# Splitting and reordering the opening of a fused Linformer attention and quick-GELU feed-forward kernel, and moving one later projection

## Chip, cores, metric

One core of a Trainium2 chip. The metric is the device time of one execution in microseconds (us), median of several runs. The span of a profile (first to last instruction) is some 1.8 us shorter than the time of the same run. All runs used here are of the fast state, but for run 5, a single run whose state is unknown; each also lists the mean clock that the matrix engine (PE) was granted.

## The reference

Eight batches, eight heads, 1024 tokens, head size 64; k and v are projected along the sequence to 64 rows.

```python
k_proj = einsum('ks,bhsd->bhkd', E, k)
v_proj = einsum('ks,bhsd->bhkd', F, v)
attn   = softmax(q @ k_proj.T / sqrt(64))
x      = (attn @ v_proj)            # heads side by side: 8192 x 512
h      = x @ w_in                   # 512 -> 2048
out    = (h * sigmoid(1.702 * h)) @ w_out
```

## The kernel before

The output is made in 16 blocks of 512 tokens. For each block, `ffn1` runs 16 chunks (`fc`) of the first matrix, `ffn2` four row groups of the second. The attention of later blocks is filled in between, by a table of slots: `at(j, slot, f)` runs `f` after chunk `slot` of block `j`; `O` = 16 is the first slot of the `ffn2` part. Two places matter: the opening, ahead of the first `ffn1`, and the projections of batch 3 in block 3.

```python
nc.sync.dma_start(out=ef_f[:KP], in_=E)
nc.scalar.dma_start(out=ef_f[KP:], in_=F)
load_kv(k, kt, 0, "k_sb", H // 2)              # GpSimd queue, fp32 -> bf16
...
load_kv(q, qt, 0, "q0_sb", H, 0, 2)
load_kv(v, vt, 0, "v_sb", ((0, 4), (4, 2), (6, 2)))
load_kv(q, qt, 0, "q0_sb", H, 2, 2)
for i in range(6):
    load_w_in(i)
...
def proj(b):                                   # reads k_sb and v_sb of batch b
    ...
def kv_out(b):
    def go():
        ...
        nc.vector.tensor_copy(k_b, ps[LO])
        if b > 1:
            nc.sync.dma_start_transpose(out=kts[b % 2], in_=k_b...)   # k' for the scores
        v_out(b, ps, 0, HP)
...
def warm(n):                                   # matmuls on zeros: keep PE's clock up
    w_ps = f_tile([P, TB])
    for _ in range(n):
        nc.tensor.matmul(w_ps, zeros[:, :P], zeros, start=True, stop=True)
...
at(2, O + 5, sums(4))                          # reciprocals, out to DRAM, broadcast back
at(3, 6, proj(3), kv_out(3), values(4, 0))
...
for j in range(3, NBLK - 1):
    for u in range(2):
        if j + 3 < NBLK:
            at(j, O + 6 * u, scores(j + 3, u)) # block 3: first use of k' of batch 3
...
for j in range(NBLK):
    if j % NB2 == 0 and j // NB2 + 2 < B:
        load(j // NB2 + 2)                     # k, q, v of a later batch into single buffers
```

The buffers of the loaded k, q and v are single. So the loads of a later batch wait for the reads of the one before.

The softmax here doesn't subtract the row's maximum and nothing guards it: scores larger than these inputs give would overflow.

Of the kernel before, what the change touches and what calls it, by code (L numbers as in the profile page):

```python
# [10 lines left out]
BF16 = mybir.dt.bfloat16  # L11
AF = mybir.ActivationFunctionType
# [5 lines left out]
def kernel(ctx, tc, q, k, v, E, F,  # L18
# [5 lines left out]
    P = 128  # L24
# [55 lines left out]

    nc.sync.dma_start(out=ef_f[:KP], in_=E)
    nc.scalar.dma_start(out=ef_f[KP:], in_=F)
    load_kv(k, kt, 0, "k_sb", H // 2)
    ident = consts.tile([P, P], BF16)
    make_identity(nc, ident)
    load_kv(q, qt, 0, "q0_sb", H, 0, 2)
    load_kv(v, vt, 0, "v_sb", ((0, 4), (4, 2), (6, 2)))
    load_kv(q, qt, 0, "q0_sb", H, 2, 2)
    for i in range(6):
        load_w_in(i)  # L90
    load_kv(q, qt, 0, "q0_sb", H, JB, JB)
    for i in range(6, 8):
# [14 lines left out]
    ones = consts.tile([P, D], BF16)  # L107
    nc.vector.memset(ones, 1.0)

    vxs = []  # L110
    for i in range(2):
        vx = consts.tile([P, H, D + 1], BF16, name=f"vx{i}")
        nc.vector.memset(vx, 0.0)
        for r, xs_ in ((LO, X_LO), (HI, X_HI)):
            nc.vector.memset(vx[r].rearrange("k (u x) d -> k u x d", x=4)[:, :, xs_, D:], 1.0)
        vxs.append(vx)

    def f_tile(shape, dt=F32):
        return ps_f.tile(shape, dt, name="f_ps")

    def warm(n):
# [3 lines that stand above are left out]
# [1 line left out]
    warm(12)  # L126
    nc.vector.tensor_copy(ef_sb[:, :S // 2], ef_f[:, :S // 2])
    nc.scalar.copy(ef_sb[:, S // 2:], ef_f[:, S // 2:])
    eft = consts.tile([P, J, 2 * KP], BF16, name="eft")
    efv = ef_sb.rearrange("k (p j) -> k j p", j=J)  # L130
    t_ps = f_tile([P, J, 2 * KP], BF16)
    for j in range(J):
        nc.tensor.transpose(t_ps[:, j, :], efv[:, j, :], ident)
    nc.vector.tensor_copy(eft, t_ps)
    warm(4)


    kvps, kbs, qT, expT, xT, rbc = {}, {}, {}, {}, {}, {}
# [1 line left out]
    def proj(b):  # L140
        def go():
            kvps[b] = f_tile([P, H, D])
            for j in range(J):
                for e, r in enumerate((LO, HI)):
                    nc.tensor.matmul(kvps[b][r], eft[:, j, e * KP:(e + 1) * KP],  # L145
                                     (kt, vt)[e][b][:, :, j, :],
                                     start=(j == 0), stop=(j == J - 1))
        return go

    def proj0(e, h0, n):  # L150
        ps = f_tile([P, n, D])
        for j in range(J):
            nc.tensor.matmul(ps, eft[:, j, :], (kt, vt)[e][0][:, h0:h0 + n, j, :],  # L153
                             start=(j == 0), stop=(j == J - 1))
        return ps

    def k_half(k_ps, g):
        k_b = att.tile([KP, H // 2, D], BF16, name="k0_b")
        nc.vector.tensor_copy(k_b, k_ps[LO])
        k_tr(0, k_b, 2 * g)  # L160

    def k_tr(b, k_b, p0):
        n = k_b.shape[1] // 2
# [3 lines left out]
                                ident[:KP, :KP])  # L167
        nc.vector.tensor_copy(kts[b % 2][:, p0:p0 + n, :], t_ps)

    def v_out(b, v_ps, p0, n, cp=nc.vector.tensor_copy):  # L170
        if b < 2:
            if n == 1:
                for r, t in ((LO, p0 % 2), (HI, 1 - p0 % 2)):
                    cp(vxs[b][r, 2 * p0 + t, :D], v_ps[HI, t, :])
            else:
                vv = v_ps[HI].rearrange("k (u x) d -> k u x d", x=4)
                vx = vxs[b][:, 2 * p0:2 * (p0 + n), :D].rearrange("k (u x) d -> k u x d", x=4)
                for r, xs_ in ((LO, X_LO), (HI, X_HI)):
                    cp(vx[r, :, xs_], vv[:, :, xs_])
        if b > 0:  # L180
            vv = v_ps[HI].rearrange("k (u x) d -> k u x d", x=4)
            for r, xs_ in ((LO, X_LO), (HI, X_HI)):
                nc.vector.tensor_copy(vqs[b % 2][r].rearrange("k (u e) d -> k u e d", e=2), vv[:, :, xs_, :])

    def kv_out(b):
        def go():
            ps = kvps.pop(b)
            k_b = att.tile([KP, H, D], BF16, name="k_b")
            nc.vector.tensor_copy(k_b, ps[LO])  # L189
            if b > 1:  # L190
                nc.sync.dma_start_transpose(out=kts[b % 2], in_=k_b.rearrange("k h d -> k (h d)"))
            v_out(b, ps, 0, HP)
            kbs[b] = k_b
        return go

    def q_tr(b, g):
        def go():
            if g == 0:
                qT[b] = att.tile([P, J, HP, P], BF16, name="qT")
            t_ps = f_tile([P, 2, HP, P], BF16)  # L200
            for jj in range(2):
                for h in range(H):
                    r = h % 2 * D
                    nc.tensor.transpose(t_ps[r:r + D, jj, h // 2, :], qt[0][:, h, 2 * g + jj, :], ident)  # L204
            nc.vector.tensor_copy(qT[b][:, 2 * g:2 * g + 2], t_ps)
        return go

    def q_dma(b, j0=0, n=J):
# [16 lines left out]
    def scores(h, u, half=None):  # L225
        b, c = divmod(h, NB2)
        j0, n = (c * JB, JB) if half is None else (c * JB + half * JB // 2, JB // 2)
        ts = slice(j0 * P - c * TB, (j0 + n) * P - c * TB)

        def go():  # L230
            if h not in expT:
                expT[h] = att.tile([P, HP, TB], BF16, name="expT", bufs=3)
            s_ps = [f_tile([P, n * P]) for _ in range(2)]
            eight(s_ps, [kts[b % 2][:, 2 * u + i, :] for i in range(2)],
                 [qT[b][:, j0:j0 + n, 2 * u + i, :] for i in range(2)])
            for i in range(2):
                nc.scalar.activation(expT[h][:, 2 * u + i, ts], s_ps[i], AF.Exp, scale=scale)  # L237
        return go
# [54 lines left out]
    def tok(h, p, half):  # L293
        def go():
            d_ps = f_tile([P, 4, D + 1]) if (h, half) == (0, 0) and p > 1 else                 ps_d.tile([P, 4, D + 1], F32, name="d_ps")
            for i in range(2):
                t = 2 * half + i
                nc.tensor.matmul(d_ps[:, 2 * i:2 * i + 2, :].rearrange("s t d -> s (t d)"),  # L298
                                 expT[h][:, p, t * P:(t + 1) * P],
                                 vxs[h // NB2][:, 2 * p:2 * p + 2].rearrange("r t d -> r (t d)"),  # L300
                                 start=True, stop=True)
            rd = work.tile([P, 4, 1], F32, name="rd")
            nc.vector.reciprocal(rd, d_ps[:, :, D:])
            xs[h, p, half] = work.tile([P, 4, D], BF16, name="x_sb", bufs=4)
            nc.vector.tensor_tensor(xs[h, p, half], d_ps[:, :, :D], rd.to_broadcast([P, 4, D]), op=ALU.mult)  # L305
        return go
# [14 lines left out]
    def ffn1(j, fc, ts=slice(0, TB)):  # L321
        if j not in gts:
            gts[j] = work.tile([P, FC, TB], BF16, name="gT")
        n = ts.stop - ts.start
        h_ps = f_tile([P, n])
        for kc in range(KC):
            nc.tensor.matmul(h_ps, w_in_sb[:, kc, fc * P:(fc + 1) * P], xT[j][:, kc, ts],  # L327
                             start=(kc == 0), stop=(kc == KC - 1))
        if j > 0 or ts.start > 0 or fc > 3:
            nc.scalar.activation(gts[j][:, fc, ts], h_ps, AF.Gelu_apprx_sigmoid)  # L330
        else:

            t_sb = work.tile([P, n], F32, name="t_sb", bufs=3)
            nc.scalar.activation(t_sb, h_ps, AF.Tanh, scale=0.851)
            g = gts[j][:, fc, ts]
            nc.vector.scalar_tensor_tensor(g, t_sb, 1.0, h_ps, op0=ALU.add, op1=ALU.mult)
            nc.vector.tensor_scalar_mul(g, g, 0.5)
# [32 lines left out]
    def at(j, slot, *fs):  # L370
        fill.setdefault((j, slot), []).extend(fs)

    O = FC
    Q = 2 * FC
    for g in range(2):
        k_half(proj0(0, 4 * g, 4), g)
        warm(3)
    q_tr(0, 0)()
    warm(2)
    v_out(0, proj0(1, 0, 4), 0, 2)  # L380
    for u in range(2):
        scores(0, u, 0)()
    for p in range(2):
        tok(0, p, 0)()
    v_out(0, proj0(1, 4, 2), 2, 1)
    x_tr(0, 0, 0)()
    v_out(0, proj0(1, 6, 2), 3, 1, nc.scalar.copy)
    tok(0, 2, 0)()
    x_tr(0, 1, 0)()
    tok(0, 3, 0)()  # L390
    x_tr(0, 2, 0)()
    q_tr(0, 1)()
    x_tr(0, 3, 0)()

    order = [(half, fc) for fcs in (range(12), range(12, FC)) for half in range(2) for fc in fcs]
    at(0, 0, scores(0, 0, 1))
    at(0, 1, scores(0, 1, 1))
    for p in range(HP):
        at(0, 5 + p, tok(0, p, 1))
        at(0, 8 + p, x_tr(0, p, 1))  # L400
    at(0, 20, q_tr(0, 2))
    at(0, 23, q_tr(0, 3))
    at(0, 3, gelu_table)
    for u in range(2):
        at(0, Q + u, scores(1, u))
    at(0, Q + 1, gelu_table)
# [20 lines left out]
    at(2, 11, norm(3, 1))  # L427
    at(2, O + 5, sums(4))
    at(2, O, q_dma(3))
    at(3, 6, proj(3), kv_out(3), values(4, 0))  # L430
    for b in range(4, B):
        j = NB2 * b - 4
        at(j, O + 6, proj(b), kv_out(b))
# [59 lines left out]
```

## Time and profile before

| | before |
|---|---|
| median time, us | 513.48 (512.97 to 514.33, 4 runs) |
| span of the profile | 513.4 |
| PE busy | 497.8 us, 97% |
| PE idle | 6.2 us in the first 30 us; 9.4 us after, of which 3.2 at the very end and 1.1 in the wait below |
| PE at half clock | from 7.3 us to past 10.4 us |

A row of the stage view gives the stretch, its length, busy us (and instructions) of PE, weight loads, VectorE (DVE), ScalarE (ACT) and GpSimd (POOL), then the granted clock, the DMA share and GB/s. In a timeline row the brackets at the end say how long the engine had been idle and what ended that.

### The profile page before, as it was taken

What the parts mean: (1) busy time and instruction counts of PE and PEld (TensorE: products, weight loads), DVE (VectorE), ACT (ScalarE), POOL (GpSimd) and SP (SyncE); (2) the same over time, 40 slices, a digit from 0 to 9 for tenths busy, and PEclk for the clock granted to TensorE, in tenths of its full rate; (3) what the DMA queues carried; (4) which work ended last, traced back from release to release, by engine and by line L of the source; (5) the groups of instructions that cost most, each with busy time, mean ns of one, the idle gap of its engine ahead of it and who ended that gap; (6) DMA issues with size and microseconds to landing.
All of it is one profiled execution on the core that took longest, in us unless ns stands there. A gap on an engine that the chain in (4) does not pass through costs nothing.

```text
span 513.4 us, 7127 instructions
## 1 busy us (share of the span) xinstructions
PE 497.8 (97%) x3022; PEld 231.1 (45%) x3072; DVE 165.0 (32%) x203; ACT 262.5 (51%) x439; POOL 77.3 (15%) x96
## 2 busy tenths in 40 slices
PE   6899999999999999999999999999999999999997
PEld 3585445434434444444444444444444444444444
DVE  2542224765261621416242241615214161511000
ACT  1476454555537456372655627375473737344351
POOL 6442051060510051000510023000000000000000
PEclk8999999999999999999999999999999999999999
DMA  9999989999899389670997339990602305050102
GB/s 168 197 202 207 212 121 165 191 150 161 195 179 245 44 148 211 135 172 15 224 170 184 73 78 215 126 235 12 170 1 63 103 1 165 1 165 1 82 0 83
DMA packets 124737, 67.64 MB, mean 132 GB/s; under 512 B 92273, under 2 KB 116081, under 8 KB 122785
## 3 DMA queue, kind: packets, MB, share of 16 engines
q0 software_dynamic: 84384, 29.37, 51.0%
q1 hardware_dynamic: 40240, 37.56, 29.7%
q8 instruction: 24, 0.39, 0.3%
q10 hardware_dynamic: 80, 0.26, 0.2%
q14 instruction: 9, 0.07, 0.0%
HBM read 71.83 MB, written 16.97 MB: 173 GB/s over the span
## 4 chain that ended last, share of the span: by engine, by line
PE 93%; DMA 3%; issue 1%; DVE 1%; ACT 1%; ACTq 0%
PE f_ps L359 42%; PE f_ps L327 42%; PE f_ps L145 3%; PE f_ps L222 2%; DMA kt<-k_b 2%; PE n_ps L222 1%; DMA ef_f<-in_E_dram 1%; PE f_ps L124 1%; PE n_ps L313 1%; PE f_ps L153 1%; PE d_ps L298 1%; PE d_ps L256 1%; PE f_ps L204 0%; PE f_ps L351 0%; DVE x_sb L305 0%
## 5 line engine op out<-in xcount | busy, mean ns | idle before, releaser
L327 PE MATMUL f_ps<-xT,w_in_sb 128*128 128x512 bf16 (+1 forms) x1071 | 225.8, 366 | 1.1
L359 PE MATMUL f_ps<-w_out_sb,gT 128*128 128x512 bf16 x976 | 221.0, 379 | 4.1 <-issue 3.6
L330 ACT ACTIVATE gT<-f_ps 128x512 bf16<-128x512 f32 (+1 forms) x268 | 151.2, 575 | 64.6 <-PE f_ps L327 63.6
L327 PEld LDWEIGHTS <-w_in_sb 128*128 128x128 bf16 x1088 | 105.3, 98 | 115.8 <-issue 2.1
L359 PEld LDWEIGHTS <-gT 128*128 128x128 bf16 x1008 | 95.7, 98 | 120.4 <-issue 11.3
L362 ACT COPY o_sb<-f_ps 128x512 f32<-128x512 f32 x63 | 36.9, 586 | 128.5 <-PE f_ps L359 117.9
L286 DVE TENSOR_TENSOR xT<-n_ps,rbc 128x512 bf16<-128x512 f32 x48 | 30.9, 686 | 211.3 <-PE n_ps L222 123.0
L259 DVE RECIPROCAL rden<-d_ps 128x512 f32<-128x512 f32 x24 | 78.7, 3322 | 7.8 <-PE d_ps L256 7.8
L64 POOL DMA_DIRECT2D q_sb<-in_q_dram x56 | 49.1, 904 | 59.1 <-DMA k_sb<-in_k_dram 39.0
L237 ACT ACTIVATE expT<-f_ps 128x512 bf16<-128x512 f32 (+1 forms) x68 | 35.2, 572 | 37.7 <-PE f_ps L222 37.7
L58 POOL DMA_DIRECT2D k_sb<-in_k_dram x9 | 7.8, 863 | 172.0 <-PE f_ps L145 151.7
L237 ACT ACT_TABLE_LOAD x13 | 16.7, 1283 | 5.9 <-PE f_ps L222 5.7
L241 ACT ACT_TABLE_LOAD x14 | 18.0, 1283 | 0.3
L189 DVE CAST k_b<-f_ps 64x512 bf16<-64x512 f32 x7 | 4.8, 681 | 36.7 <-PE f_ps L145 36.7
L222 PE MATMUL f_ps<-qT,kt 64*32 64x512 bf16 (+1 forms) x272 | 13.7, 374 | 1.5 <-DMA kt<-k_b 1.1
L276 DVE RECIPROCAL rdn<-d_ps 128x512 f32<-128x512 f32 x4 | 13.4, 3352 | 5.0 <-PE d_ps L222 5.0
L145 PE MATMUL f_ps<-k_sb,eft 128*64 128x512 bf16 x56 | 13.4, 382 | 0.0
L145 PE MATMUL f_ps<-v_sb,eft 128*64 128x512 bf16 x56 | 13.4, 382 | 0.0
L353 DVE COPY o_sb<-f_ps 128x256 f32<-128x256 f32 x1 | 0.4, 425 | 38.6 <-issue 38.6
L222 PEld LDWEIGHTS <-kt 64*32 64x32 bf16 x272 | 3.9, 88 | 15.5 <-issue 13.8
L222 PE MATMUL n_ps<-expT,vq 64*32 64x512 bf16 x208 | 10.4, 378 | 0.0
L305 DVE TENSOR_TENSOR x_sb<-d_ps,rd 128x256 bf16<-128x256 f32 x22 | 9.3, 425 | 0.8
(59 smaller groups left out, 123.3 us busy)
## 6 DMA issues: line engine op xcount, KB each, us to landing
out_dram<-o_sb SPq DMA_DIRECT2D x15, 1024.0 KB
rbc<-rdr SPq DMA_DIRECT2D x24, 512.0 KB
k_sb<-in_k_dram POOLq DMA_DIRECT2D x7, 1024.0 KB, 14.2
v_sb<-in_v_dram POOLq DMA_DIRECT2D x7, 1024.0 KB, 10.4
q_sb<-in_q_dram POOLq DMA_DIRECT2D x56, 128.0 KB, 14.4
w_in_sb<-in_moe_w_in_dram POOLq DMA_DIRECT2D x8, 256.0 KB, 12.5
w_out_sb<-in_moe_w_out_dram POOLq DMA_DIRECT2D x4, 512.0 KB, 14.7
k_sb<-in_k_dram POOLq DMA_DIRECT2D x2, 512.0 KB, 7.7
```

The costliest lines, as they stand in the source:

```text
L64: nc.gpsimd.dma_start(out=qt[b][:, j], in_=qv[:, j])
L145: nc.tensor.matmul(kvps[b][r], eft[:, j, e * KP:(e + 1) * KP], (kt, vt)[e][b][:, :, j, :], start=(j == 0), stop=(j == J - 1))
L222: nc.tensor.matmul(outs[i][r.start + c:r.start + c + 32], lhsTs[i][ri, c:c + 32], rhss[i][ri], start=True, stop=True)
L237: nc.scalar.activation(expT[h][:, 2 * u + i, ts], s_ps[i], AF.Exp, scale=scale)
L241: nc.scalar.preload_act_table(AF.Gelu_apprx_sigmoid)
L259: nc.vector.reciprocal(rden[:, e, :], d_ps[e])
L276: nc.vector.reciprocal(rd, d_ps[i])
L286: nc.vector.tensor_tensor(x_of(h)[:, 2 * u + i, :], n_ps[i], rbc[h][:, 2 * u + i, :], op=ALU.mult)
L327: nc.tensor.matmul(h_ps, w_in_sb[:, kc, fc * P:(fc + 1) * P], xT[j][:, kc, ts], start=(kc == 0), stop=(kc == KC - 1))
L330: nc.scalar.activation(gts[j][:, fc, ts], h_ps, AF.Gelu_apprx_sigmoid)
L359: nc.tensor.matmul(o_ps[n], gts[j][:, fc, n * P:(n + 1) * P], w_out_sb[:, fc, :], start=(fc == 0), stop=(fc == FC - 1))
L362: nc.scalar.copy(osb[j][:, n, :], o_ps.pop(n))
```

## The change

The intent is a shorter latency chain before the first `ffn1`. The core of the diff (the mask, the tiles for v' and the q units are cut):

```diff
 nc.scalar.dma_start(out=ef_f[KP:], in_=F)
-load_kv(k, kt, 0, "k_sb", H // 2)
+nc.scalar.preload_act_table(AF.Exp)
+load_kv(k, kt, 0, "k_sb", ((0, 4), (4, 2), (6, 2)))
 ...
 load_kv(v, vt, 0, "v_sb", ((0, 4), (4, 2), (6, 2)))
+load_w_in(0)
 load_kv(q, qt, 0, "q0_sb", H, 2, 2)
-for i in range(6):
+for i in range(1, 6):
     load_w_in(i)
 ...
+def v_piece(h0, n):
+    v_ps = proj0(1, h0, n)
+    vx = vx0[0] if n == 4 else vx_of(0, h0 // 2)
+    nc.vector.tensor_tensor(vx[:, :, :D], v_ps, mask[...], op=ALU.mult)
 ...
-if j > 0 or ts.start > 0 or fc > 3:      # else tanh on ACT, two operations on DVE
+if j > 0 or ts.start > 0 or fc > 5:
 ...
-for g in range(2):
-    k_half(proj0(0, 4 * g, 4), g)
-    warm(3)
+for h0, n in ((0, 4), (4, 2), (6, 2)):
+    k_piece(h0, n)
 ...
-q_tr(0, 1)()                             # second q transpose, before the last xT copy
-at(0, 0, scores(0, 0, 1))
-at(0, 1, scores(0, 1, 1))
+at(0, 1, q_tr(1))
+at(0, 3, scores(0, 0, 1))
+at(0, 4, scores(0, 1, 1))
 ...
-at(0, 3, gelu_table)
+at(0, 5, gelu_table)
 ...
-at(3, 6, proj(3), kv_out(3), values(4, 0))
+at(3, 2, proj(3), kv_out(3), values(4, 0))
```

More of the change, by code (lines that the diff above doesn't have):

```diff
@@ L108, with vx_tile @@
     nc.vector.memset(ones, 1.0)
-    vxs = []
-    for i in range(2):
-        vx = consts.tile([P, H, D + 1], BF16, name=f"vx{i}")
+    def vx_tile(name, n):
+        vx = consts.tile([P, n, D + 1], BF16, name=name)
         nc.vector.memset(vx, 0.0)
-        for r, xs_ in ((LO, X_LO), (HI, X_HI)):
-            nc.vector.memset(vx[r].rearrange("k (u x) d -> k u x d", x=4)[:, :, xs_, D:], 1.0)
-        vxs.append(vx)
+        for p in range(n // 2):
+            for r, t in ((LO, p % 2), (HI, 1 - p % 2)):
+                nc.vector.memset(vx[r, 2 * p + t, D:], 1.0)
+        return vx
+    vx0 = [vx_tile(f"vx0{h}", n) for h, n in ((0, 4), (4, 2), (6, 2))]
+    vx1 = vx_tile("vx1", H)
+    mask = consts.tile([P, 4, D], BF16, name="mask")
+    nc.vector.memset(mask, 0.0)
+    for r, xs_ in ((LO, X_LO), (HI, X_HI)):
+        nc.vector.memset(mask[r, xs_], 1.0)
     def f_tile(shape, dt=F32):
@@ L128, with eft @@
     nc.scalar.copy(ef_sb[:, S // 2:], ef_f[:, S // 2:])
-    eft = consts.tile([P, J, 2 * KP], BF16, name="eft")
+    efts = [consts.tile([P, J // 2, 2 * KP], BF16, name=f"eft{i}") for i in range(2)]
     efv = ef_sb.rearrange("k (p j) -> k j p", j=J)
-    t_ps = f_tile([P, J, 2 * KP], BF16)
-    for j in range(J):
-        nc.tensor.transpose(t_ps[:, j, :], efv[:, j, :], ident)
-    nc.vector.tensor_copy(eft, t_ps)
-    warm(4)
+    for i, cp in enumerate((nc.vector.tensor_copy, nc.scalar.copy)):
+        t_ps = f_tile([P, J // 2, 2 * KP], BF16)
+        for j in range(J // 2):
+            nc.tensor.transpose(t_ps[:, j, :], efv[:, i * J // 2 + j, :], ident)
+        cp(efts[i], t_ps)
+    ffs = consts.tile([P, J, 2, KP], BF16, name="ffs")
+    for i in range(2):
+        nc.vector.tensor_copy(ffs[:, i * J // 2:(i + 1) * J // 2],
+                              efts[i][:, :, None, KP:].to_broadcast([P, J // 2, 2, KP]))
+    warm(2)
+    def eft(j, cols=slice(0, 2 * KP)):
+        return efts[j // (J // 2)][:, j % (J // 2), cols]
     kvps, kbs, qT, expT, xT, rbc = {}, {}, {}, {}, {}, {}
@@ L144, in go @@
                 for e, r in enumerate((LO, HI)):
-                    nc.tensor.matmul(kvps[b][r], eft[:, j, e * KP:(e + 1) * KP],
+                    nc.tensor.matmul(kvps[b][r], eft(j, slice(e * KP, (e + 1) * KP)),
                                      (kt, vt)[e][b][:, :, j, :],
@@ L152, in proj0, with k_piece @@
         for j in range(J):
-            nc.tensor.matmul(ps, eft[:, j, :], (kt, vt)[e][0][:, h0:h0 + n, j, :],
+            nc.tensor.matmul(ps, ffs[:, j].rearrange("s i k -> s (i k)") if e else eft(j), (kt, vt)[e][0][:, h0:h0 + n, j, :],
                              start=(j == 0), stop=(j == J - 1))
         return ps
-    def k_half(k_ps, g):
-        k_b = att.tile([KP, H // 2, D], BF16, name="k0_b")
+    def k_piece(h0, n):
+        k_ps = proj0(0, h0, n)
+        k_b = att.tile([KP, n, D], BF16, name=f"k0_b{h0}", bufs=1)
         nc.vector.tensor_copy(k_b, k_ps[LO])
-        k_tr(0, k_b, 2 * g)
+        warm(1)
+        k_tr(0, k_b, h0 // 2)
     def k_tr(b, k_b, p0):
@@ L168, in k_tr, with vx_of, v_out @@
         nc.vector.tensor_copy(kts[b % 2][:, p0:p0 + n, :], t_ps)
-    def v_out(b, v_ps, p0, n, cp=nc.vector.tensor_copy):
-        if b < 2:
-            if n == 1:
-                for r, t in ((LO, p0 % 2), (HI, 1 - p0 % 2)):
-                    cp(vxs[b][r, 2 * p0 + t, :D], v_ps[HI, t, :])
-            else:
-                vv = v_ps[HI].rearrange("k (u x) d -> k u x d", x=4)
-                vx = vxs[b][:, 2 * p0:2 * (p0 + n), :D].rearrange("k (u x) d -> k u x d", x=4)
-                for r, xs_ in ((LO, X_LO), (HI, X_HI)):
-                    cp(vx[r, :, xs_], vv[:, :, xs_])
-        if b > 0:
-            vv = v_ps[HI].rearrange("k (u x) d -> k u x d", x=4)
-            for r, xs_ in ((LO, X_LO), (HI, X_HI)):
-                nc.vector.tensor_copy(vqs[b % 2][r].rearrange("k (u e) d -> k u e d", e=2), vv[:, :, xs_, :])
+    def vx_of(b, p):
+        if b == 1:
+            return vx1[:, 2 * p:2 * p + 2]
+        return vx0[0][:, 2 * p:2 * p + 2] if p < 2 else vx0[p - 1]
+    def v_piece(h0, n):
+        v_ps = proj0(1, h0, n)
+        vx = vx0[0] if n == 4 else vx_of(0, h0 // 2)
+        nc.vector.tensor_tensor(vx[:, :, :D], v_ps, mask[:, h0 % 4:h0 % 4 + n], op=ALU.mult)
+    def v_out(b, v_ps):
+        vv = v_ps[HI].rearrange("k (u x) d -> k u x d", x=4)
+        for r, xs_ in ((LO, X_LO), (HI, X_HI)):
+            if b == 1:
+                vx = vx1[r, :, :D].rearrange("k (u x) d -> k u x d", x=4)
+                nc.vector.tensor_copy(vx[:, :, xs_], vv[:, :, xs_])
+            nc.vector.tensor_copy(vqs[b % 2][r].rearrange("k (u e) d -> k u e d", e=2), vv[:, :, xs_, :])
     def kv_out(b):
@@ L191, in go, with q_tr @@
                 nc.sync.dma_start_transpose(out=kts[b % 2], in_=k_b.rearrange("k h d -> k (h d)"))
-            v_out(b, ps, 0, HP)
+            v_out(b, ps)
             kbs[b] = k_b
         return go
-    def q_tr(b, g):
+    q0s = [consts.tile([P, 2, 2, P], BF16, name=f"q0T{u}") for u in range(2)]
+    def q_tr(g):
         def go():
-            if g == 0:
-                qT[b] = att.tile([P, J, HP, P], BF16, name="qT")
-            t_ps = f_tile([P, 2, HP, P], BF16)
-            for jj in range(2):
-                for h in range(H):
-                    r = h % 2 * D
-                    nc.tensor.transpose(t_ps[r:r + D, jj, h // 2, :], qt[0][:, h, 2 * g + jj, :], ident)
-            nc.vector.tensor_copy(qT[b][:, 2 * g:2 * g + 2], t_ps)
+            if 0 not in qT:
+                qT[0] = att.tile([P, J, HP, P], BF16, name="qT")
+            for u, cp in enumerate((nc.vector.tensor_copy, nc.scalar.copy)):
+                if g == 0 or u == 0:
+                    t_ps = f_tile([P, 2, 2 if g == 0 else HP, P], BF16)
+                for jj in range(2):
+                    for h in range(4 * u, 4 * u + 4):
+                        r = h % 2 * D
+                        nc.tensor.transpose(t_ps[r:r + D, jj, h // 2 - (2 * u if g == 0 else 0), :],
+                                            qt[0][:, h, 2 * g + jj, :], ident)
+                if g == 0:
+                    cp(q0s[u], t_ps)
+            if g > 0:
+                nc.vector.tensor_copy(qT[0][:, 2 * g:2 * g + 2], t_ps)
         return go
@@ L234, in go @@
             eight(s_ps, [kts[b % 2][:, 2 * u + i, :] for i in range(2)],
-                 [qT[b][:, j0:j0 + n, 2 * u + i, :] for i in range(2)])
+                 [q0s[u][:, :, i, :] if (b, j0, n) == (0, 0, 2) else qT[b][:, j0:j0 + n, 2 * u + i, :]
+                   for i in range(2)])
             for i in range(2):
@@ L299, in go @@
                                  expT[h][:, p, t * P:(t + 1) * P],
-                                 vxs[h // NB2][:, 2 * p:2 * p + 2].rearrange("r t d -> r (t d)"),
+                                 vx_of(h // NB2, p).rearrange("r t d -> r (t d)"),
                                  start=True, stop=True)
@@ L374 @@
     Q = 2 * FC
-    for g in range(2):
-        k_half(proj0(0, 4 * g, 4), g)
-        warm(3)
-    q_tr(0, 0)()
-    warm(2)
-    v_out(0, proj0(1, 0, 4), 0, 2)
+    for h0, n in ((0, 4), (4, 2), (6, 2)):
+        k_piece(h0, n)
+    q_tr(0)()
+    warm(1)
     for u in range(2):
         scores(0, u, 0)()
+    warm(2)
+    v_piece(0, 4)
     for p in range(2):
         tok(0, p, 0)()
-    v_out(0, proj0(1, 4, 2), 2, 1)
+    v_piece(4, 2)
     x_tr(0, 0, 0)()
-    v_out(0, proj0(1, 6, 2), 3, 1, nc.scalar.copy)
     tok(0, 2, 0)()
     x_tr(0, 1, 0)()
+    v_piece(6, 2)
+    x_tr(0, 2, 0)()
     tok(0, 3, 0)()
-    x_tr(0, 2, 0)()
-    q_tr(0, 1)()
     x_tr(0, 3, 0)()
     order = [(half, fc) for fcs in (range(12), range(12, FC)) for half in range(2) for fc in fcs]
-    at(0, 0, scores(0, 0, 1))
-    at(0, 1, scores(0, 1, 1))
+    at(0, 1, q_tr(1))
+    at(0, 3, scores(0, 0, 1))
+    at(0, 4, scores(0, 1, 1))
     for p in range(HP):
-        at(0, 5 + p, tok(0, p, 1))
+        at(0, 6 + p, tok(0, p, 1))
         at(0, 8 + p, x_tr(0, p, 1))
-    at(0, 20, q_tr(0, 2))
-    at(0, 23, q_tr(0, 3))
-    at(0, 3, gelu_table)
+    at(0, 20, q_tr(2))
+    at(0, 23, q_tr(3))
+    at(0, 5, gelu_table)
     for u in range(2):
```

## The prediction

> **What bounds the kernel now.** I read the page first, then the busy time of the engines by stage, then the chain of waits of the first 40 us, and last the timeline and the DMA issues of the same stretch.
>
> ```profile
> span 513.4 us, 7127 instructions
> PE 497.8 (97%) x3022; PEld 231.1 (45%) x3072; DVE 165.0 (32%) x203; ACT 262.5 (51%) x439; POOL 77.3 (15%) x96
> PEclk8999999999999999999999999999999999999999
> ...
> 5.30:7.30 2.00, 0.00 (x0) 0.00 (x0) 0.43 (x1) 1.73 (x2) 2.00 (x3) 0.99 1.09 161
> 7.30:9.00 1.70, 1.47 (x10) 1.18 (x11) 0.36 (x1) 0.17 (x1) 1.54 (x3) 0.50 1.15 188
> ...
> 10.80:11.50 0.70, 0.63 (x6) 0.31 (x4) 0.04 (x1) 0.00 (x0) 0.46 (x1) 1.00 1.64 195
> ...
> 22.26:513.00 490.74, 481.59 (x2885) 221.98 (x2932) 156.98 (x176) 257.86 (x428) 64.22 (x74) 1.00 0.80 130
> ```
>
> The matrix engine (PE) is busy 97%. From the first feed-forward matmul at 22.26 us to the end it is busy 481.59 of 490.74 us (98%), at full clock; the change alters nothing in that work except the order within its first 8 us. So all there is to win lies in the 22 us opening (4.3% of the span), and the whole program can only move by the amount by which the feed-forward stream starts earlier, less what its first pieces lose. In the stage rows (stretch, its length, then busy PE, PEld, DVE, ACT, POOL, clock, DMA) PE does nothing from 5.30 to 7.30 and then runs at clock 0.50 until after 10.4.
>
> The chain of waits says what the opening is made of:
>
> ```profile
> 0.74 4.75 DMA ef_f<-in_E_dram
> ...
> 5.56 1.28 ACT L128
> 6.84 0.01 issue
> 6.85 0.63 ACT ef_sb L128
> 7.48 0.05 issue
> 7.53 1.07 PE f_ps L133 x8
> 8.60 1.71 PE f_ps L124 x4
> 10.31 1.13 PE f_ps L153 x8
> ...
> 22.46 0.38 ACT xT L315
> ...
> 30.02 0.30 DVE xT L315
> 30.32 0.04 issue
> 30.36 3.76 PE f_ps L327 x33
> ```
>
> E and F land at 5.49; the exp table load (1.28) stands between them and the cast; then transposes, warming matmuls, and a serial chain k, q, scores, v', x up to the last xT copy, which ends at 22.84. The first half of the feed-forward block then runs until the last xT copy of the second half, 30.32, and only from 30.36 is PE fed without gaps.
>
> Is it compute or data that is late? The last field of the DMA rows is us from issue to landing:
>
> ```profile
> k_sb<-in_k_dram POOLq DMA_DIRECT2D x1, 512.0 KB, 6.7
> ...
> q_sb<-in_q_dram POOLq DMA_DIRECT2D x1, 256.0 KB, 8.8
> ...
> v_sb<-in_v_dram POOLq DMA_DIRECT2D x1, 512.0 KB, 10.4
> ...
> w_in_sb<-in_moe_w_in_dram POOLq DMA_DIRECT2D x1, 256.0 KB, 12.8
> ...
> 16.34 0.74 POOL L79 DMA_DIRECT2D w_in_sb<-in_moe_w_in_dram  x1 [0.58 <-DMA v_sb<-in_v_dram]
> ```
>
> Added to the issue times of the timeline: k's first half 1.24 + 6.7 = 7.9, its second 2.0 + 8.6 = 10.6, q 3.40 + 8.8 = 12.2, v's first part 4.30 + 10.4 = 14.7, the others 16.0 and 17.3, the next q pair 18.7, first w_in chunk 7.31 + 12.8 = 20.1, then 22.5, 23.5, 24.9, 26.2 and the sixth 16.34 + 11.2 = 27.5. Their consumers start at 10.1, 12.8, 15.2, 16.2, 18.4, 19.3 and 22.3: everything waits 1.3 to 3 us for compute. The opening is bound by latency of small operations, with the DMA stream a little ahead.
>
> **What the Trainium skill says.** "ScalarE: Activation LUTs", What ACT_TABLE_LOAD costs, gives about 1283 ns for a load whatever the set; the trace agrees (1.28). "TensorE: Matmul & The Clock Gate", Part 1, says that the array runs at half clock until it has been busy for a window of about 3.4 us, and that the window is free-running. The trace agrees: half clock from 7.3 to between 10.4 and 10.8, one window after a pause of 2 us. "VectorE: DVE Perf Modes", the perf-mode tier table, puts a tensor_tensor with a PSUM operand at one element per cycle; the trace has 128x256 at 0.42 us, the same as a cast of 256 columns out of PSUM (0.42), so the mask multiply costs one ordinary eviction. "DMA: Bandwidth & Descriptors", Issuing engines are not separate DMA queues, says that all issuers share the same 16 engines. That fits the trace, where 256 KB pieces land one after another about 1.3 us apart: a load that moves forward pushes another back, and no total gets shorter.
>
> **The change part by part**, as a new clock for the opening. Durations are rows of the trace before.
>
> *Exp table at once.* 1.28 leaves the path: ACT casts at 5.56 for 0.62, transposes at 6.23 instead of 7.53.
>
> *eft in halves, warm 4 to 2.* Four transposes and a 512-column eviction (about 0.42, estimated between 0.29 for 256 and 0.69 for 1024 columns); the second half on ACT (about 0.6) is ready near 7.5 instead of 9.33. The F-twice copies add two vector operations (about 0.3 each, estimated) in time when DVE idles. The first k projection can now start when k lands, 7.9, instead of 10.1.
>
> *k pieces.* Four heads: matmuls 1.04, cast 0.42, transposes 0.23, eviction 0.23. Each two-head piece: matmuls 0.61, cast 0.30, transpose 0.2, eviction 0.2. From 7.95 the first piece lets PE go at 9.7, the second at 10.85; the third also waits for its data (10.6) and ends near 12.0. Before, kt was complete at 14.80.
>
> *q by units.* q lands at 12.2, now the wait: transposes 12.3 to 12.9, unit 0 evicted by DVE near 13.05, unit 1 by ACT near 13.5. Scores at 13.1 and 13.55, four exponentials (1.21) done by 14.8. Before, the scores started at 17.2.
>
> *v' by mask.* v's first part lands at 14.7, so again data decides: 1.04 of matmuls and one multiply of 0.42 instead of two casts of 0.60 together give v' at 16.2 instead of 17.9. The gain so far is 1.7, no longer 4: DMA has eaten the rest. Then, by the spacings before (first reciprocal 0.33 after the matmuls start, x 0.22 later and 0.42 long, the next x 0.54 later): x0 at 17.2, x1 at 17.8, v' of pair 2 at 18.0, x2 at 19.0, v' of pair 3 at 19.35, x3 at 20.35, transpose 0.3 and ACT copy 0.37: last xT copy at about 21.1 instead of 22.84. Gain 1.75.
>
> *w_in sooner.* Its first chunk swaps places with a q pair of equal size: 18.7 instead of 20.1, enough for a start before 21. The chunks after it stay where they were.
>
> *What is given back.* The second q transpose (16 transposes, 0.57 of PE in the chain) used to lie ahead of the last xT copy in time that PE partly idled; now it sits after fc 1 on a busy PE: +0.57. Its eviction (0.69) now stands on DVE behind the gelu work of fc 0 and 1 (0.60 a piece, spacing of the rows), so the scores after fc 3 are asked for 1.9 after fc 0 and their data is ready at 2.3: about +0.45. fc 4 and 5 also change from ACT's gelu to tanh plus two DVE operations: 2 x 0.60 = 1.2 more on DVE. From fc 0 to the last xT copy DVE has 6 x 0.60 + 0.65 + 4 x 0.55 (reciprocal and x) + 4 x 0.21 (copies) = 7.3 us, starting 0.4 after fc 0, so at best 7.7, where before the stretch from fc 0 done (23.17) to PE's resumption (30.36) took 7.2. With small PSUM-buffer stalls I get 8.2. Thus fc 0 is done at 21.1 + 0.33 = 21.4 and PE resumes at 29.2 (best) to 29.7, against 30.36.
>
> Sum: 1.75 won, 0.6 to 1.1 given back: about 0.9 us of 513.7, that is 512.8. Weights for later stages don't bind: the seventh and eighth w_in chunks land by 33.0 and are wanted after 35, the w_out chunks land 2 us or more ahead of use.
>
> **The rivals.** *The w_in stream becomes the bound.* fc 10 starts at 28.85 before and its chunk lands at 27.5; fc 2 at 24.36 and its chunk at 22.5. Slack is 1.3 to 1.9, so even a much faster compute chain gains no more than 1.2 to 1.3: 512.4. For it: DMA is at 9 tenths throughout. Against: my vector chain ends later. *DVE gives everything back.* If the scores wait longer for the q eviction, or the exponentials meet the table load, PE resumes at 30.3 as before: 513.7, or slightly slower. *The clock.* PE's pause shrinks from 2.3 to about 1 us, so the half-clock window may vanish. If it stays, the k projections run at half rate, k ends 0.6 to 1 later, but q's and v's landing absorbs most: 0.25 at the end, 513.05. If it vanishes, nothing beyond my sum, since data is then the wait. *The naive hope*, adding the removed 1.28, 1.8 and 0.9 to 4 us or more (509.7), fails on the landing times of q and v.
>
> **Range and chances.** The centre is 512.8; 511.8 would be the w_in limit plus a lucky run, 513.8 no gain at all; the three runs before spread over 1.4 us, so these ends include 0.4 of noise. 2% is 10.3 us, half of the whole opening, and no rival reaches it in either direction: faster 0.01, within 2% 0.98, slower 0.01.
>
> **What would show it.** Right: ACT's table load before 3 us; first k matmul near 8; the q transposes idle until the DMA of q at about 12.3, and the first v matmul idle until about 14.8; last first-half xT copy near 21.1; scores of the second half waiting for the DVE eviction; DVE nearly full from 22 to 29.5; gap-free PE from about 29.5. Wrong: PE matmuls of fc 2 to fc 10 waiting for w_in (the stream binds), k's first matmuls already waiting past 9 (E and F land late), or a later feed-forward stage whose idle time differs, since I take everything after 30 us as a plain shift.

## More of the kernel before

The prediction shows the lines of the opening. There is one more that it did not weigh, from the waits of PE in the kernel before (total us, times, longest):

```profile
PE f_ps L222 <- DMA kt<-k_b: 1.1, 1, 1.1
```

It is a single wait, at 141 us, of the scores of block 6 for the transposed k' of batch 3.

## The result

| | before | after |
|---|---|---|
| median time, us | 513.48 (4 runs) | 519.51 (518.06 to 520.63, 4 runs) |
| ratio of fast runs | | 1.0114, 95% interval 1.0085 to 1.0144 |
| span of the profile | 513.4 | 516.3 |

A ratio is the mean time of one kernel's fast runs over that of the other's fast runs of the same rounds, so it is not quite the ratio of the medians. The change costs 6 us; the prediction had 512.8, with 513.8, no gain at all, as its upper end. A second series of the unaltered changed kernel (below) gave 1.0113.

The page of the changed kernel, whose lines answer to those of before (the third is the head of the chain that ended last):

```profile
span 516.3 us, 7210 instructions
PE 504.4 (98%) x3076; PEld 231.2 (45%) x3076; DVE 167.5 (32%) x227; ACT 263.4 (51%) x439; POOL 78.0 (15%) x97
PE 92%; DMA 4%; DVE 1%; ACT 1%; issue 1%; SPq 0%; POOLq 0%
```

DMA in the chain rose from 3% to 4%. First the opening, from its chain of waits, timeline and stage rows:

```profile
1.25 7.00 DMA k_sb<-in_k_dram
...
20.72 0.37 ACT L349 COPY xT<-n_ps 128x256 bf16<-128x256 bf16 x1 [0.84 <-PE n_ps L347]
...
20.00:22.26 2.26, 1.86 (x10) 1.10 (x10) 0.62 (x2) 0.76 (x2) 1.49 (x2) 0.63 1.46 196
22.26:25.00 2.74, 2.64 (x33) 1.90 (x33) 1.93 (x6) 1.06 (x4) 1.48 (x2) 0.69 1.45 196
...
30.68 0.30 DVE xT L349
30.98 0.04 issue
31.03 3.76 PE f_ps L361 x33
```

The chain starts at k's data, and the last xT copy of the first half ends at 21.09 (predicted 21.1). But PE's clock is at 0.63 and 0.69 in the two stretches from 20.00 to 25.00, and PE runs without gaps only from 31.03, against 30.36 before. That is 0.7 us of the 2.9 by which the spans differ. Per 10 us, PE's busy time from there on is complete in the changed kernel but for one stretch, 140 to 150. The waits of PE name it:

```profile
PE f_ps L255 <- DMA kt<-k_b: 3.3, 1, 3.3
```

2.2 us more than before: 0.7 and 2.2 make the 2.9. The timeline around it, first of the kernel before, then of the changed one (SPq is the sync engine's queue, here issuing; a POOL row is an issue by GpSimd):

```profile
128.89 1.32 SPq L264 DMA_DIRECT2D rbc<-rdr  x2
...
131.66 0.88 POOL L58 DMA_DIRECT2D k_sb<-in_k_dram  x1 [18.61 <-PE n_ps L222]
131.84 3.72 SPq L191 DMA_TRANSPOSE kt<-k_b  x1
...
138.05 1.29 DVE L286 TENSOR_TENSOR xT<-n_ps,rbc 128x512 bf16<-128x512 f32 x2 [5.33 <-DMA rbc<-rdr]
...
142.12 0.41 PE L222 MATMUL f_ps<-qT,kt 64*32 64x512 bf16 x8 [1.11 <-DMA kt<-k_b]
```

```profile
128.85 1.32 SPq L298 DMA_DIRECT2D rbc<-rdr  x2
128.87 0.88 POOL L58 DMA_DIRECT2D k_sb<-in_k_dram  x1 [15.14 <-PE n_ps L255]
...
130.91 2.02 SPq L216 DMA_TRANSPOSE kt<-k_b  x1
...
139.58 1.29 DVE L320 TENSOR_TENSOR xT<-n_ps,rbc 128x512 bf16<-128x512 f32 x2 [9.65 <-DMA rbc<-rdr]
...
145.01 0.41 PE L255 MATMUL f_ps<-qT,kt 64*32 64x512 bf16 x8 [3.34 <-DMA kt<-k_b]
```

With the projections four chunks earlier, the transpose of k' is issued only 0.93 us earlier: it stands in the sync queue behind the broadcast of reciprocals (rbc) and the output store, which did not move. The bulk load of the next k, which waits for the projections to have read their k (the row names the matmuls just behind them), starts 2.8 us earlier. Both transfers of the sync queue are then used later: the broadcast, issued at the same 128.9, 1.5 us later, and the transpose 14.1 us after its issue instead of 10.2.

That made theory M: the moved projections let the bulk loads of batch 4 loose on the DMA engines just ahead of a transpose that PE needs. Its rival, theory C: the half clock in the opening is the loss, and the wait near 142 us merely varies from run to run.

### The profile page after: what moved, and what is told of

It is laid out like the page before. It is cut to its first block, busy times and chain, and to the rows that moved or that the text cites. A ratio compares the mean times of both kernels' runs of the same rounds, so it can differ in the third digit from the quotient of the medians.

```text
span 516.3 us, 7210 instructions
## 1 busy us (share of the span) xinstructions
PE 504.4 (98%) x3076; PEld 231.2 (45%) x3076; DVE 167.5 (32%) x227; ACT 263.4 (51%) x439; POOL 78.0 (15%) x97
## 4 chain that ended last, share of the span: by engine, by line
PE 92%; DMA 4%; DVE 1%; ACT 1%; issue 1%; SPq 0%; POOLq 0%
PE f_ps L393 42%; PE f_ps L361 41%; DMA kt<-k_b 3%; PE f_ps L164 3%; PE f_ps L255 2%; DMA k_sb<-in_k_dram 1%; PE n_ps L255 1%; PE n_ps L347 1%; PE f_ps L172 1%; PE f_ps L233 1%; PE d_ps L290 1%; PE d_ps L332 0%; DVE x_sb L339 0%; PE f_ps L385 0%; ACT expT L271 0%
## 5 line engine op out<-in xcount | busy, mean ns | idle before, releaser
L393 PE MATMUL f_ps<-w_out_sb,gT 128*128 128x512 bf16 x1008 | 227.2, 380 | 0.0
```

The costliest lines, as they stand in the source:

```text
L393: nc.tensor.matmul(o_ps[n], gts[j][:, fc, n * P:(n + 1) * P], w_out_sb[:, fc, :], start=(fc == 0), stop=(fc == FC - 1))
```

## The experiments

Eleven runs, all correct. Ratios are against the kernel before on the same chip.

| run | median us | ratio, 95% interval |
|---|---|---|
| projections put back | 514.17 | 1.0011 (0.9991 to 1.0031) |
| projections alone moved | 518.33 | 1.0090 (1.0068 to 1.0113) |
| loads of batch 4 held back | 514.02 | 1.0011 (0.9993 to 1.0030) |
| put back, opening kept warm | 515.03 | 1.0023 (1.0004 to 1.0041) |
| changed kernel, second trace | 520.39 (one run) | |
| moved alone, wait filled | 517.28 | 1.0078 (1.0062 to 1.0094) |
| front of the opening only | 513.17 | 0.9996 (0.9982 to 1.0011) |
| front only, loads held back | 513.11 | 0.9993 (0.9980 to 1.0007) |
| changed kernel, second series | 519.61 | 1.0113 (1.0088 to 1.0138) |
| changed, warm and filled | 517.81 | 1.0085 (1.0070 to 1.0100) |
| front only, k' of batch 3 turned by PE | 513.07 | 0.9990 (0.9976 to 1.0004) |

### 1. The projections put back

```diff
 # changed kernel
-at(3, 2, proj(3), kv_out(3), values(4, 0))
+at(3, 6, proj(3), kv_out(3), values(4, 0))
```

> The changed kernel with one thing undone: the projections of batch 3 stand again after chunk 6 of block 3, not after chunk 2. Theory M (the moved projections): most of the 6 us come from them, because the read of k ends 2.8 us earlier, the bulk loads of batch 4 start that much earlier, and the transpose of k' (which the sync queue holds back until 130.9) shares the DMA engines with them. Then this kernel is back within 1.5 us of the kernel before, 513 to 515, and the wait of the scores for that transpose near 142 us is about 1 us or less. Theory C (the clock in the opening): the loss is the half-clock window near 20 to 24 us and the wait near 142 us only varies from run to run. Then this kernel stays at 517 or more.

514.17, ratio 1.0011: theory M. The transpose is no longer among the waits of PE's matmuls in its trace. Nearly all of the loss is gone with this one line, although the whole opening of the change is still in. The opening itself is not distinguishable from no effect.

### 2. The projections alone moved

```diff
 # kernel before
-at(3, 6, proj(3), kv_out(3), values(4, 0))
+at(3, 2, proj(3), kv_out(3), values(4, 0))
```

> The kernel before with only the projections of batch 3 moved from chunk 6 to chunk 2. Theory M: 517 to 519, with a wait of 3 us or more for the transpose of k' near 142 us, and the broadcast of the reciprocals landing about 1.5 us later than in the kernel before. Theory C: no change, 513 to 514.

518.33, ratio 1.0090: the move alone makes 4.6 of the 6 us. The two effects add up to 1.0101, short of the 1.0113 of the whole but within the intervals. The six clocks are 0.999, 0.997, 0.996, 0.993, 0.996 and 0.993, and the times rise as they fall, from 516.47 to 520.04. From the waits of PE, and then the chain of the opening (as to code that of the kernel before), both in the trace of the 516.47 run, which had no half-clock window:

```profile
PE f_ps L222 <- DMA kt<-k_b: 3.9, 1, 3.9
...
7.32 13.71 DMA w_in_sb<-in_moe_w_in_dram
...
28.57 0.30 DVE xT L315
...
28.91 3.76 PE f_ps L327 x33
```

The second part was a surprise. Without a half-clock window, the old opening waits for the first w_in chunk (to 21.03) and PE is gap-free from 28.91, not from 30.36. The trace on which I built the prediction was one with such a window. The wait of 3.9 us was not followed by half clock in this trace.

### 3. The loads of batch 4 held back

```diff
 # changed kernel, projections at chunk 2
 for j in range(NBLK):
     if j % NB2 == 0 and j // NB2 + 2 < B:
+        if j == 4:
+            nc.gpsimd.tensor_copy(gate, kts[1][:, 0, :1])   # waits for the transposed k'
         load(j // NB2 + 2)
```

> The changed kernel, projections at chunk 2 as in it, with one tiny GpSimd copy that reads the transposed k' ahead of the loads of batch 4, so that these loads are issued only once the transpose has landed. If the bulk loads are what delays the transpose, it lands at 136 to 141 us instead of 145, the wait near 142 us is gone and the time is 513 to 515 (as with the projections put back, or a little better). If the transpose is slow by itself, or behind its own queue's 2 MB, it still lands near 144 to 145 and the time is 518 or more. A danger: the loads come 10 us later and a later block could wait for q of batch 4.

514.02: the loss is gone with the projections still at chunk 2. From its timeline, the copy that the landing of the transpose releases, and the scores:

```profile
139.17 0.19 POOL L488 COPY gate<-kt 128x1 bf16<-128x1 bf16 x1 [25.93 <-DMA kt<-k_b]
...
140.91 0.41 PE L255 MATMUL f_ps<-qT,kt 64*32 64x512 bf16 x8
```

Issued at 130.26, the transpose landed by 139.17, within 8.9 us. It stood behind the same broadcast and the same store. So neither its place in its own queue nor its own work makes it late. The DMA queues (packets, MB, share of the engines' time) in the same stretch, 128.9 to 139 us, of the changed kernel and of this one:

```profile
q1 hardware_dynamic: 576, 1.31, 43.8%
q0 software_dynamic: 636, 0.65, 40.6%
```

```profile
q1 hardware_dynamic: 976, 2.16, 67.8%
```

q1 carries the broadcast, the store and the transpose, q0 the bulk loads. In 10.1 us, q0 took 636 packets of about 1 KB and q1 got 576 of about 2.3 KB; alone, q1 moved 2.16 MB (run 3 is 0.65 us ahead in this stretch). The kernel before had 2.02 MB on q1 and 0.07 on q0 in these 10.1 us.

### 4. The opening kept warm

Seven warming matmuls in the pauses of the opening, projections put back:

```diff
 # changed kernel, projections at chunk 6
     v_ps = proj0(1, h0, n)
+    if n == 4: warm(2)
 ...
 x_tr(0, 0, 0)()
+warm(2)
 tok(0, 2, 0)()
 ...
 tok(0, 3, 0)()
+warm(3)
 x_tr(0, 3, 0)()
```

> The changed kernel with the projections put back (as the first run) and seven more warming matmuls, two behind the first v' projection, two and three in the two pauses before the last values of the opening. If PE's half-clock window near 20 to 24 us comes from the pauses between 16 and 20.4 us, it is gone here, PE runs without gaps from about 29.8 us instead of 31.0, and the time is 1 to 1.5 us below the first run. If VectorE's queue is the bound there, the clock stays whole but the time moves by under 0.4 us.

515.03, ratio 1.0023: a miss. It is not faster than run 1 but 0.9 us slower in the median, with overlapping intervals, and PE is gap-free from 30.14. The reason: run 1 had no half-clock window in its trace either (gap-free from 29.94), and a clock of 0.999 or 1.0 in five of six runs. There was next to nothing to cure in these runs. At full clock the changed opening still has its other waits, among them:

```profile
23.61 0.30 PE L255 MATMUL f_ps<-qT,kt 64*32 64x256 bf16 x8 [0.39 <-DVE qT L238]
```

This row of run 1 is the wait for the second q eviction in VectorE's queue that the prediction had.

### 5. The changed kernel once more, for a second trace

No edit.

> The changed kernel once more, unaltered, for a second trace. Its timed runs show a clock of 0.993 where the trace shows 0.996. If the wait near 142 us, once it lasts a few us, sends PE to half clock, a trace with a time of 519 or more shows a stretch of clock 0.5 in the 10 us after 142; if the half clock belongs to the opening alone, it shows two such stretches before 30 us and full clock after 142.

520.39, clock 0.993. Its stage rows:

```profile
20.50:23.50 3.00, 3.00 (x27) 2.02 (x28) 1.12 (x4) 1.14 (x3) 1.84 (x3) 0.50 1.46 198
...
142.00:144.00 2.00, 0.00 (x0) 0.00 (x0) 0.00 (x0) 0.00 (x0) 0.00 (x0) 1.00 2.51 149
...
146.00:148.00 2.00, 2.00 (x29) 0.67 (x6) 1.70 (x3) 1.86 (x3) 1.76 (x2) 0.69 2.43 155
148.00:150.00 2.00, 2.00 (x7) 0.68 (x5) 2.00 (x1) 0.71 (x3) 0.00 (x0) 0.50 2.44 162
150.00:152.00 2.00, 2.00 (x11) 0.88 (x10) 2.00 (x2) 0.38 (x1) 0.00 (x0) 0.96 1.87 176
```

Both stretches that I had set against each other are there. PE stands still (this wait is 3.9 us), and then the clock is at half: 1.24 us of the first stretch after (0.31 / 0.5 x 2), 2.0 of the next, 0.16 of the third, together 3.4 us, hence 1.7 us lost on top of the wait. A second window lies in the opening.

### 6. The move alone, with the wait filled

```diff
 # kernel before, projections at chunk 2
+at(3, O, lambda: warm(16))      # ahead of the scores that wait
 at(3, O, scores(6, 0))
```

> The kernel before with the projections of batch 3 at chunk 2 (518.3) and 16 warming matmuls (3.5 us) directly ahead of the scores that wait for the transposed k'. They fill the wait and add nothing to it. If the wait itself (3 to 4 us) is all of the loss, the time stays at 518. If about half of the loss is the half clock that follows such a pause, it falls to 516 to 517 and the clock of the runs is 0.997 or more.

517.28, ratio 1.0078 against 1.0090: some 0.6 us better, less than I expected, inside the intervals and on another chip. The clock is 0.999 or 1.0 in four of the five runs; the fifth, the profiled one (518.34), has 0.996, and its trace shows half clock in the old opening as in the kernel before (0.50 from 9.0 to 10.7; gap-free from 30.59) and full clock after the wait. The trace still shows 0.6 us of waiting behind the 3.6 us of warming, so the wait is about 4 us long, and it is most of the loss.

### 7. The front of the opening only

From the kernel of run 1, everything behind v' is put back: order of loads, second q transpose before the last xT copy, scores at slots 0 and 1, gelu table at 3, tanh for four chunks, not six.

```diff
 # changed kernel, projections at chunk 6
-load_w_in(0)
 load_kv(q, qt, 0, "q0_sb", H, 2, 2)
-for i in range(1, 6):
+for i in range(6):
 ...
 tok(0, 3, 0)()
+q_tr(1)()
 x_tr(0, 3, 0)()
 ...
-at(0, 1, q_tr(1))
-at(0, 3, scores(0, 0, 1))
-at(0, 4, scores(0, 1, 1))
+at(0, 0, scores(0, 0, 1))
+at(0, 1, scores(0, 1, 1))
 ...
-if j > 0 or ts.start > 0 or fc > 5:
+if j > 0 or ts.start > 0 or fc > 3:
```

> Only the front of the change: exp table at once, eft in halves, k pieces, q by units, v' by mask. Order of loads, place of the second q transpose, scores, tanh count and the projections of batch 3 as in the kernel before. If what was won in front was given back by the second q transpose and the two more tanh pieces on VectorE, PE runs without gaps from about 28.9 us (the first w_in chunk lands at 21) instead of 29.9 to 30.3, and the time is about 1 us below that of the changed kernel with the projections put back: 512.5 to 513.5, at or just under the kernel before. If the front itself is no gain, 514 or more.

513.17, ratio 0.9996, and from the chain of waits:

```profile
28.72 3.76 PE f_ps L360 x33
```

28.72 is 1.2 us ahead of run 1 (29.94) and 0.2 ahead of the old opening at full clock (28.91). One trace is not sharp here: runs 8 and 11, with the same opening and full clock, have 29.66 and 28.60; in run 8 the w_in chunk that the chain waits for landed at 26.60, in run 7 at 25.68. All three still lie ahead of the changed opening at full clock (29.93 to 30.33 in runs 1, 3 and 9). What the changed kernel gives back behind the first `ffn1` is thus real in the traces, and no gain of the front alone over the old opening at full clock, of which there is one trace, is shown. In time, 0.9996 against 1.0011 points the same way, with overlapping intervals and on different chips.

### 8. The front only, loads held back

Run 7 plus the edit of run 3.

> As the run before, plus the tiny GpSimd copy that holds back the loads of batch 4 until the transposed k' of batch 3 has landed. If the wait near 142 us (0 to 1.1 us where the projections stand at chunk 6) is worth something, 0.3 to 1 us below the run before and less spread; if not, the same. It is my candidate for a kernel that beats both: 512 to 513.

513.11, ratio 0.9993: not distinguishable from the kernel before or from run 7. With the projections at chunk 6, holding back the loads buys nothing.

### 9. The changed kernel, second series

No edit; on the chip of the two runs below.

> The changed kernel unaltered, with five rounds on one chip with the two runs below. Expected 519 to 520, clock 0.993 in most runs: a half-clock window (3.4 us at half rate, 1.7 us lost) after the wait near 142 us in nearly every run, and one near 20 us in many. If the clock is 0.996 or more in most runs, the half clock near 20 us was a matter of the chip and the time is 517 to 518.

519.61, ratio 1.0113. The clocks of its six runs are 0.996, 0.993, 1.0, 0.997, 0.993 and 0.993, against 0.997 to 1.0 (mean 0.999) of the kernel before. The one run at 1.0 took 516.64. The trace of this series had its half clock after the wait (4.3 us long) and none in the opening, so the latter comes and goes with the same code. So does the former: the first trace of the changed kernel, with a wait of 3.3 us, and that of run 2, with 3.9, had full clock behind it. The wait, and the queues from 128.9 to 139 us, in this trace:

```profile
PE f_ps L255 <- DMA kt<-k_b: 4.3, 1, 4.3
...
q0 software_dynamic: 1028, 1.03, 73.7%
q1 hardware_dynamic: 449, 0.89, 27.1%
```

### 10. The changed kernel, opening warm and wait filled

The edits of runs 4 and 6 together, projections at chunk 2.

> The changed kernel with the projections left at chunk 2, the seven warming matmuls in the pauses of the opening and sixteen ahead of the scores that wait near 142 us. No pause is left in which PE could fall to half clock, the wait itself stays. If the half clock is worth what its windows say (up to 2 x 1.7 us), 516 to 517.5 and a clock of 0.999 or 1.0 in nearly all runs; if only the wait counts, as much as the run above.

517.81, a little above the range, with a clock of 0.999 or 1.0 in all four runs. Against run 9 on the same chip 1.8 us are gone. The clocks say about the same: (1 - 0.9953) x 517.7 = 2.4 us at most lost to the clock in run 9 on average, (1 - 0.9990) x 511.7 = 0.5 in the kernel before. The other 4.3 us (517.81 - 513.54) stay: the wait, filled or not, and the opening. That split is not sharp: the one run of run 9 at full clock lost only 3.1 us (516.64 - 513.54), and whether the added matmuls cost something of their own (run 4 was 0.9 us above run 1) is not separated.

### 11. The front only, k' of batch 3 turned by PE

```diff
 # kernel of run 7
-if b > 1:
+if b > 1 and b != 3:
     nc.sync.dma_start_transpose(out=kts[b % 2], in_=k_b...)
 ...
 at(3, 6, proj(3), kv_out(3), values(4, 0))
+at(3, 9, lambda: k_tr(3, kbs[3], 0))
```

> The front of the change alone (513.17 in its run) with the k' of batch 3 transposed by four PE transposes at chunk 9 instead of a DMA transpose. PE has 0.2 to 0.4 us more to do, and no DMA stands before the scores near 142 us any more. If that wait still costs something in timed runs where the projections stand at chunk 6, 512.3 to 513; if it costs nothing there, 513 to 513.7.

513.07, ratio 0.9990, the lowest of all and still not outside the noise. No version here beats the kernel before clearly.

## Why the prediction was wrong

The step that failed is the one that limits the change to the opening: "the change alters nothing in that work except the order within its first 8 us", and once more at the end, "I take everything after 30 us as a plain shift". One line of the diff moved the projections of batch 3, and the prediction does not mention it. A later stage whose idle time differs was on its list of signs of being wrong, and that sign came: a wait of 3.3 us near 142 us. The moved line cost 4.6 us alone (run 2), and putting it back recovered all but 0.6 (run 1). The cause is shown, not only argued, by run 3: with that line still moved and only the loads held back, the loss is gone. What carries it is the sharing of the DMA engines: with the loads beside it, q1's bytes fell from 2.16 to 1.31 MB. The Trainium skill, "DMA: Bandwidth & Descriptors", Queues, rings and completion order, says that each DMA engine serves its queues in turn, packet by packet. The fall fits this, but the packet counts of the profile do not show how the turns went: 636 (q0) against 576 (q1) in the first trace of the changed kernel, 1028 against 449 in run 9, with the same code.

Of the loss of 6 us, run 10 leaves 4.3 as the wait of about 4 us plus what the opening gives back, and takes away 1.8, which the clocks put down to half clock: in a window after that wait in some runs and in one of the opening in some (run 5 has both). With the one full-clock run of run 9 the first part would be 3.1. Run 2 and run 1 give 4.6 for the move and 0.6 for the opening; the rest, some 0.8 us, lies within the intervals. How much of the opening's part is its order and how much its half-clock windows stays open: the interval of run 1 includes no effect at all.

For the opening, point by point:

- *Table load, eft, k, q and v pieces*: right in time. The last xT copy ended at 21.09 (predicted 21.1); the transposes of q, at 12.35, and the first v' matmul, at 14.85, came within 0.1 us of the forecast. But the wait for data that was to set these times was only part of it: the transposes of q followed k's last piece without a pause, and at 14.85 the last exponential (ended 14.84) and v's data came together. That the sum fits so closely is luck in part.
- *What is given back*: right in kind, too small in size. At full clock PE was gap-free from 29.94 (run 1) to 30.33 (run 3), not from 29.2 to 29.7, though the last xT copy of the first half ended at 20.91 and 21.31, close to the forecast.
- *The start from which I counted*: wrong. I set the new opening against 30.36, from a trace with a half-clock window between 7.3 and 10.7. At full clock the old opening ends at 28.91 (run 2), because its first w_in chunk decides there, and its last xT copy ends at 21.38, not 22.84. So the gain of the front, 1.75 in the prediction, is 0.1 to 0.5 against that trace, and the changed opening loses about 1 us to it. In the eleven runs of the kernel before in the series of runs 1 to 4, eight had a clock of 0.999 or more. A hint was at hand: the profiled run had taken 515.17 us, and the three others 512.97 to 514.33.
- *The rival of the clock*: I put it in the old place, at the k projections. It appeared at 20 to 24 us instead, after a stretch in which PE was busy about half the time, in two of the three traces of the changed kernel, and in neither run 1 nor run 3, which have the same opening and the same pauses.
- *The w_in stream as the bound*: not in the changed kernel, but it bounds the old opening at full clock (run 2) and the front-only kernel in runs 7 and 8. So "The opening is bound by latency of small operations" held for the old opening with a half-clock window (the trace that I had, and run 6), not without one.

## What to carry to other kernels

Read every line of a diff for what it releases, not only for what it does: moving a reader earlier frees its buffer earlier, and the loads that were waiting may then compete with a small transfer that the critical engine needs soon. A small transfer behind a fixed queue gets little earlier with its producer (0.93 us here, where the loads came 2.8 us earlier); either hold the bulk load back until it has landed, or leave both where they were. And before pricing the gain of a few us, check that the trace at hand is typical of the timed runs, in its clock and in its time.

## What the Trainium skill lacked or had wrong

- "TensorE: Matmul & The Clock Gate", Part 1, gives an idle window of about 3.4 us as what brings half clock; a later section of the page tells of a kernel whose frequent short idles do it, without a length. Here a window of half clock also followed pauses that were shorter: after 2.3 us without matmuls in the kernel before (clock 0.50 from 7.3 to past 10), and, in run 5, after a stretch of 3.0 us in which PE was busy for 1.63 us. Run 1 had the same 1.63 us and kept full clock. Nor did every pause of that length bring it: 3.9 us did in run 5 and not in run 2. The length of the half-clock stretch, 3.4 us in run 5, agrees with the page.
- "DMA: Bandwidth & Descriptors", Queues, rings and completion order, names the turn-taking by packets but not what it means for a small transfer beside bulk loads: from its issue to its landing or use, the transpose of k' took up to 8.9 us alone with its own queue's traffic, 10.2 with loads issued at the same moment, and 13.3 to 14.5 with loads issued 2.0 to 3.9 us before it (four traces).
- "TensorE: Matmul & The Clock Gate", Part 1, says that the number of slow matmuls at the start varies from run to run. It does not say that a later half-clock window comes and goes with the same code, so that a single trace may hold one that most timed runs do not have: 513.4 us of span at clock 0.996 in the trace before, where the series of runs 1 to 4 had spans from 510.8 to 513.6 for the same kernel, eight of eleven at 0.999 or 1.0.
